# Top-k attention and a channel mixer on one core: all results turned back by the vector engine, match replacements written in place, one share of products moved in tail steps

## The chip, the cores and the metric

The kernel runs on one core of a Trainium2 chip. A core has a matrix engine (TensorE, here PE), a vector engine (VectorE, DVE), a scalar engine (ScalarE, ACT), a general engine (GpSimd, POOL), a queue that issues DMAs (SyncE, SP), and 16 DMA engines that all queues share. Each engine works through its own instructions in the order in which they were written; engines wait for one another by semaphores. The metric is the time of one execution on the device in microseconds (us). The kernel before takes 1773.88 us, the median of three runs (1771.52 to 1775.6).

## The reference

The inputs are q, k and v of 8 batches, 8 heads, 576 positions and 64 dimensions, and four weights U, V, w_ch1 and w_ch2, which arrive as float64. All the rest is float32.

```
scores = q @ k.T / 8                          # per batch and head, 576 x 576
kth    = the 32nd largest of each row
attn   = softmax over the entries >= kth      # the others count as 0
x      = attn @ v, heads side by side         # (8, 576, 512)
u      = x + (x.T @ U @ V).T                  # U: 576 x 32, V: 32 x 576
out    = u + relu(u @ w_ch1) @ w_ch2          # 512 -> 2048 -> 512
```

## The kernel before

**Steps.** Two heads of a batch form a group g, so there are 32 groups, four to a batch. The 576 rows of a group are cut into four tiles of 128 rows and a tail of 64 rows; the tails of the two heads share one tile. A step n is one tile t of one group: t = 0 to 3 are full steps with two chunks of 128 x 576 scores (one for each head), t = 4 is the tail step with one chunk. A batch is 20 steps, 16 full and 4 tail; in all there are 160.

**What a step does on DVE.** `front` finds the 32 largest of each row of each chunk. It takes the eight largest with `max` (line 385), and then three times overwrites those eight with a very negative number (`match_replace`, line 395) and takes the next eight (line 399). Each `match_replace` writes a new tile "rr" of which there are three buffers; a full step needs six. On the engine a replacement is two instructions, the load of the eight values and the replacement itself. In full steps from the 30th on, DVE also turns the second head's weights in blocks of 32 x 32 into a tile y (`blocks`, line 446). Four DMAs carry y to a scratch tile "away" in device memory (line 452) and one brings it back as part of the tile PT (line 456), so that it is fully transposed. The first head's weights are transposed on PE (line 474), whose results ACT copies into PT (lines 475 and 480).

**The other engines in a step.** ACT copies scores from PSUM to the tile Ssb and takes exponentials (line 351). POOL masks chunks (lines 402, 403 and 421). PE multiplies: scores (`scores`, lines 320 and 333, for the step that follows), weights with v (`values`, lines 498, 508 and 512; tile O), and four times a batch the mixing over positions (`mixed`, lines 533 to 566), which gives the tile uT.

**The channel products.** When a batch's four groups are mixed, `mlp(b)` is put in the list `fillers`. It is a generator that issues the matmuls of both channel products, one at a time (lines 581 and 600), and is advanced by `fill()`. Each call of `fill` adds a share to an account `due` and issues matmuls until the account is used up. The share is 1 in full steps and 0.65 in tail steps, and eight calls in each step use up one batch's products in 20 steps. So the products of batch b run among the attention steps of batch b + 1, and those of the last batch run alone at the end. The order of PE, ACT, DVE and POOL is the order of the calls in the main loop (from line 701 on): nothing is reordered there. The issues of SP are placed by the framework's scheduler.

**Where the results leave.** A batch's products are made for two spans of rows, of 320 and of 256, and for each span as four tiles "oT" of 128 channels. That makes eight tiles a batch, called tile 0 to tile 7 below. ACT copies a tile from PSUM (line 615) and POOL adds uT (line 616). Then `turned_back` transposes it, as rows of the output are positions and rows of oT are channels. It is put off in the list `late`: to the tenth matmul of the next tile, or to the fourth result of the next span, and for tile 7 to the moment at which the generator of that batch ends, with nothing put between. In the kernel before, batches 0 to 6 are turned on PE (line 648, two or three transposes a tile), ACT copies the result to "ob" (lines 650 and 652), and one or two DMAs write it (lines 654 and 659). Seven of the eight tiles of the last batch are turned by DVE instead, in blocks of 32 x 32 (line 630). There the DMAs put the blocks in place, 12 of them for a tile of 320 columns and 8 for one of 256 (lines 635 and 640), with pieces of 128 bytes in device memory.

**A main-loop step after the first batch** has this order (lines 775 to 807): four fills, with the PE transposes of the weights of an earlier step among them, `values(n - 2)`, `scores(n + 1)`, the first replacement round on DVE, a fill, the second round, the issue of y, two fills, the third round, and a last fill.

Of the kernel before, what the change touches and what calls it, by code (L numbers as in the profile page):

```python
# [8 lines left out]
F32 = mybir.dt.float32  # L9
# [17 lines left out]
def kernel(  # L27
# [29 lines left out]
    B, H, S, D = q.shape  # L57
    P = 128
# [3 lines left out]
    NF, NC = F // P, C // P  # L62
    NT, TAIL = 4, 64
# [19 lines left out]
    attn = ctx.enter_context(tc.tile_pool(name="attn", bufs=2))  # L83
# [11 lines left out]
    SPAN = ((0, 2 * P + TAIL), (2 * P + TAIL, S))  # L95
# [30 lines left out]
    def rows(t):  # L126
        return P if t < NT else TAIL
# [221 lines left out]
    def weigh(chunk, E, nmax, total=None):  # L349

        nc.scalar.activation(E, chunk, AF.Exp, bias=nmax, scale=SCALE, accum_out=total)  # L351

    def ways(g, t):

        if (g, t) == (NPAIR - 1, NT - 1):
            return (0,), (), (1,)
        if (g, t) == (NPAIR - 1, NT):
            return (0,), (), ()  # L360
        return (), (1,) if t < NT else (), (0,)
# [4 lines left out]
    def front(g, t):  # L366

        if t == 0:
            dens[g] = small.tile([P, 2 * NT + 1], F32, tag="den", name="den", bufs=3)
        chunks, den = S2s.pop((g, t)), dens[g]
        n = len(chunks)
        E2 = attn.tile([P, 2 * S], F32, tag="E", name="E", bufs=3)
        Es = [E2[:, c * S : (c + 1) * S] for c in range(n)]
        sums = [den[:, 2 * t + c : 2 * t + c + 1] for c in range(n)]
        probs[g, t] = E2
        curs, ms = list(chunks), [None] * n
        first = small.tile([P, 2, 8], F32, tag="first", name="first", bufs=3)  # L380
        nmax = small.tile([P, 2], F32, tag="nmax", name="nmax", bufs=4)
        order = (1, 0) if n == 2 else (0,)
        for c in order:
            ms[c] = first[:, c]
            nc.vector.max(ms[c], curs[c])  # L385
        yield
        early, pooled, gaps = ways(g, t)
        for i in range(1, TOPK // 8):
            if i == 1:
                nc.scalar.mul(nmax[:, 0:n], first[:, 0:n, 0], -SCALE)  # L390
                for c in early:
                    weigh(chunks[c], Es[c], nmax[:, c : c + 1])
            for c in order:
                nxt = attn.tile([P, S], F32, tag="rr", name="rr", bufs=3)
                nc.vector.match_replace(nxt, ms[c], curs[c], NEG)  # L395
                curs[c] = nxt
            for c in order:
                ms[c] = small.tile([P, 8], F32, tag="m8", name="m8", bufs=8)
                nc.vector.max(ms[c], curs[c])  # L399
            yield  # L400
        for c in pooled:
            nc.gpsimd.tensor_scalar(Es[c], chunks[c], ms[c][:, 7:8], NEG, ALU.is_lt, ALU.mult)  # L402
            nc.gpsimd.tensor_tensor(chunks[c], chunks[c], Es[c], ALU.add)  # L403
        for c in early:
            nc.vector.scalar_tensor_tensor(
                out=Es[c],
                in0=chunks[c],
                scalar=ms[c][:, 7:8],
                in1=Es[c],
                op0=ALU.is_ge,  # L410
                op1=ALU.mult,
                accum_out=sums[c],
            )
        if t == NT:
            del qkTs[g]
        yield
        for c in gaps:
            least = small.tile([P, 1], F32, tag="least", name="least", bufs=3)
            nc.scalar.mul(least, ms[c][:, 7:8], WIDEN)
            nc.scalar.activation(Es[c], chunks[c], AF.Relu, bias=least, scale=-WIDEN)  # L420
            nc.gpsimd.tensor_tensor(chunks[c], chunks[c], Es[c], ALU.subtract)  # L421
            yield
        ahead = pooled if shared(g, t) else ()
        for c in ahead:
            weigh(chunks[c], Es[c], nmax[:, c : c + 1], sums[c])
            yield
        for c in order:
            if c not in early and c not in ahead:
                weigh(chunks[c], Es[c], nmax[:, c : c + 1], sums[c])
        if t == NT and g != NPAIR - 1:  # L430
            nc.scalar.activation(den, den, AF.Identity, bias=eps)
        yield

    def shared(g, t):


        return t < NT and g * CH + t >= ROUNDED
# [183 lines left out]
    def turned_back(b, chunks, lo, c, oT):  # L621


        def run():
            cs = slice(c * P, (c + 1) * P)
            if b == B - 1 and (lo, c) != (SPAN[1][0], NC - 1):

                w = sum(rows(t) for t in chunks)
                ob = mlpp.tile([P, 3 * P], F32, tag="ob", name="ob", bufs=2)
                nc.vector.transpose(ob[:, 0:w], oT[:, 0:w])  # L630
                for a in range(4):
                    cs = slice(c * P + a * BLK, c * P + (a + 1) * BLK)
                    ba = ob[a * BLK : (a + 1) * BLK]
                    for t in chunks[0:2]:
                        nc.sync.dma_start(
                            out[b, 0:MAIN, cs].rearrange("(m i t) c -> t i m c", i=BLK, t=NT)[t],
                            ba[:, OFF[t] - lo : OFF[t] - lo + P].rearrange("i (m c) -> i m c", c=BLK),
                        )
                    if NT in chunks:
                        nc.sync.dma_start(  # L640
                            out[b, MAIN:S, cs].rearrange("(m i) c -> i m c", i=BLK),
                            ba[:, 2 * P : 2 * P + TAIL].rearrange("i (m c) -> i m c", c=BLK),
                        )
                return
            tp = ps_t.tile([P, 3, P], F32, tag="tp", name="tp")
            for i, t in enumerate(chunks):
                n = rows(t)
                nc.tensor.transpose(tp[0:n, i, :], oT[:, OFF[t] - lo : OFF[t] - lo + n], ident)  # L648
            ob = mlpp.tile([P, 3, P], F32, tag="ob", name="ob", bufs=2)
            nc.scalar.copy(ob[:, 0:2], tp[:, 0:2, :])  # L650
            if NT in chunks:
                nc.scalar.copy(ob[0:TAIL, 2], tp[0:TAIL, 2, :])
            t = chunks[0]
            nc.sync.dma_start(
                out[b, 0:MAIN, cs].rearrange("(p t) c -> p t c", t=NT)[:, t : t + 2, :],
                ob[:, 0:2],
            )
            if NT in chunks:
                nc.sync.dma_start(out[b, MAIN:S, cs], ob[0:TAIL, 2])

        return run
# [11 lines left out]
    def fill(k=1):  # L673


        nonlocal due
        for _ in range(k):
            if passes:
                passes.pop(0)()
            if mixing and next(mixing[0], True):  # L680
                mixing.pop(0)
            due += share * (SHORT if t == NT else 1) * (EARLY if n <= 2 * ALONE + 2 else 1)
            while due > 0:
                if not fillers:
                    due = 0.0
                    break
                done = next(fillers[0], None)
                if done is None:
                    fillers.pop(0)
                else:  # L690
                    due -= done
# [3 lines left out]
    t = 0  # L695
# [5 lines left out]
    for n in range(STEPS + 2):  # L701
        g, t = divmod(n, CH)
        if n < STEPS:
            if t == 0 and g + 1 < NP:
                load(g + 1)
            if t == 1 and g + 1 < NP:
                ready = prep(g + 1)
            fronts[n] = front(g, t)
            next(fronts[n])
# [70 lines left out]
            next(last)  # L780
        fill()
        next(turning, None)
        fill()
        if ease:
            next(last, None)
        if n - 2 >= ALONE:
# [17 lines left out]
        if t in (1, 3):  # L804
            next_params(1)
        next(here, None)
        fill()
    while mixing or fillers:
        fill()

# [30 lines left out]
```

## Time and profile before

| | before |
|---|---|
| time, median of three runs | 1773.88 us |
| span of the profiled execution | 1773.6 us |
| PE busy | 1669.3 us, 94% |
| DVE busy | 1560.3 us, 88% |
| ACT busy | 1029.4 us, 58% |
| POOL busy | 846.8 us, 48% |
| replacements on DVE (line 395) | 864, 742 ns each |
| transposes of results on PE (line 648) | 142, 25.3 us together |
| copies of them on ACT (lines 650, 652) | 85, 28.5 us together |
| transposes of results on DVE (line 630) | 7, 3.4 us together |

Shares of busy time mix stages, so they are read by stretches of the span. Until about 240 us the first batch's attention runs without channel products, with DVE busy 39.1 to 39.6 of each 40 us from 40 us on, and PE 19 to 36. From about 440 to 1632 us attention and channel products run together. From there to the end PE works alone on the last batch's products. A group of the profile is named by line, engine and operation, then the tile that is written and those that are read ("rr<-m,rr"); "mean ns" is the duration of one instruction. In the list of waits, "A <- B: 2.9, 4, 1.0" says that the instructions at A waited for B 2.9 us in all, in 4 waits, the longest 1.0.

### The profile page before, as it was taken

To read this page: it belongs to the slowest core of one execution; us is meant where nothing else is said; L and a number is where in the kernel's file an instruction comes from. 1 tells how busy PE (TensorE), PEld (TensorE's weight loads), DVE (VectorE), ACT (ScalarE), POOL (GpSimd) and SP (SyncE) were. 2 spreads that over 40 slices of the span, in tenths; PEclk is the share of its full clock that TensorE was granted. 3 is DMA by queue.
4 is the path that set the end of the run, shared out by engine and by line. 5 is a ranking of instruction groups with operands and counts; after the bars stand their busy time and mean duration, and the time that the engine had idled before them with its cause. 6 is when DMAs were issued, how large, how long until landed. Compare 5 with 4: busy or idle time off the path is not lost.

```text
span 1773.6 us, 28992 instructions
## 1 busy us (share of the span) xinstructions
PE 1669.3 (94%) x9851; PEld 1257.5 (71%) x9851; DVE 1560.3 (88%) x3106; ACT 1029.4 (58%) x2682; POOL 846.8 (48%) x591
## 2 busy tenths in 40 slices
PE   4666789999999999999999999999999999999999
PEld 2434556677777877788777877788777877788677
DVE  7999989899999999999999999999999999994000
ACT  4778777555656656565656656565656656564100
POOL 4777677535354554545445454444445444453000
PEclk7687799999999999999999999999999999999999
DMA  3222332222223332222233232232233232211010
GB/s 95 88 82 73 88 85 61 50 59 71 58 67 80 66 72 56 67 68 64 64 71 79 62 70 62 65 70 63 63 73 80 59 73 60 53 50 45 4 15 13
DMA packets 275829, 112.79 MB, mean 64 GB/s; under 512 B 173920, under 2 KB 260192, under 8 KB 275680
## 3 DMA queue, kind: packets, MB, share of 16 engines
q1 hardware_dynamic: 274624, 110.68, 26.4%
q8 instruction: 77, 1.26, 0.3%
q14 instruction: 72, 0.59, 0.1%
q10 hardware_dynamic: 1056, 0.26, 0.1%
HBM read 74.15 MB, written 36.70 MB: 63 GB/s over the span
## 4 chain that ended last, share of the span: by engine, by line
PE 75%; DVE 16%; POOL 4%; ACT 3%; issue 2%; DMA 1%; SPq 0%; POOLq 0%; DVEq 0%
PE mm L581 25%; PE mm L600 24%; DVE rr L395 7%; PE sc L333 6%; PE O L512 6%; DVE m L399 6%; PE tp L474 3%; DVE first L385 2%; PE sc L320 2%; PE O L498 2%; PE up L556 1%; PE O L508 1%; POOL E L402 1%; PE up L558 1%; PE tp L648 1%
## 5 line engine op out<-in xcount | busy, mean ns | idle before, releaser
L399 DVE MAX8 m<-rr 128x8 f32<-128x576 f32 x864 | 614.7, 748 | 5.5
L600 PE MATMUL mm<-hT,w 128*128 128x256 f32 (+1 forms) x2048 | 547.4, 410 | 0.0
L581 PE MATMUL mm<-uT,w 128*128 128x256 f32 (+1 forms) x2048 | 541.5, 410 | 0.9 <-ACT hT L593 0.9
L402 POOL TENSOR_SCALAR E<-Ssb,m 128x576 f32<-128x576 f32 x127 | 281.1, 2214 | 411.7 <-DVE m L399 409.1
L581 PEld LDWEIGHTS mm<-uT,w 128*128 128x128 f32 x2048 | 371.7, 190 | 115.1 <-issue 26.0
L600 PEld LDWEIGHTS mm<-hT,w 128*128 128x128 f32 x2048 | 368.3, 190 | 106.8 <-issue 22.5
L395 DVE MATCH_REPLACE8 rr<-m,rr 128x576 f32<-128x576 f32 x576 | 427.2, 742 | 0.0
L421 POOL TENSOR_TENSOR Ssb<-Ssb,E 128x576 f32<-128x576 f32 x159 | 225.4, 1418 | 122.3 <-ACT E L420 121.7
L351 ACT ACTIVATE E<-Ssb,nmax 128x576 f32<-128x576 f32 x288 | 223.3, 776 | 52.4 <-POOL Ssb L403 34.9
L593 ACT ACTIVATE hT<-mm 128x320 f32<-128x320 f32 (+1 forms) x256 | 105.1, 411 | 240.4 <-PE mm L581 240.1
L385 DVE MAX8 first<-Ssb 128x8 f32<-128x576 f32 x288 | 203.3, 742 | 31.4 <-ACT Ssb L346 31.4
L395 DVE MATCH_REPLACE8 rr<-first,Ssb 128x576 f32<-128x576 f32 x288 | 211.8, 742 | 0.0
L403 POOL TENSOR_TENSOR Ssb<-Ssb,E 128x576 f32<-128x576 f32 x127 | 179.3, 1412 | 10.6
L333 PE MATMUL sc<-qkT 64*128 64x288 f32 x1024 | 170.6, 454 | 6.7 <-ACT Ssb L344 5.8
L474 PE MATMUL tp<-ident,E 128*128 128x128 f32 x736 | 116.0, 283 | 37.1 <-ACT XT L521 14.6
L512 PE MATMUL O<-PT,va 128*64 128x128 f32 x2048 | 146.3, 284 | 1.9 <-DMA PT<-away 1.9
L474 PEld LDWEIGHTS tp<-ident,E 128*128 128x128 f32 x736 | 92.1, 145 | 68.7 <-ACT XT L521 16.6
L475 ACT COPY PT<-tp 128x512 f32<-128x512 f32 x184 | 106.6, 585 | 49.0 <-PE tp L474 46.4
L512 PEld LDWEIGHTS O<-PT,va 128*64 128x64 f32 x2048 | 113.7, 140 | 19.0 <-DMA PT<-away 2.9
L420 ACT ACTIVATE E<-Ssb,least 128x576 f32<-128x576 f32 x159 | 123.3, 776 | 5.2
L333 PEld LDWEIGHTS sc<-qkT 64*128 64x128 f32 x1024 | 93.3, 198 | 45.3 <-issue 14.3
L613 DVE TENSOR_TENSOR oT<-uT,mm 128x320 f32<-128x320 f32 (+1 forms) x8 | 3.6, 455 | 137.1 <-PE mm L600 137.1
(81 smaller groups left out, 1574.0 us busy)
## 6 DMA issues: line engine op xcount, KB each, us to landing
away<-y SPq DMA_DIRECT2D x416, 64.0 KB, 1.8
PT<-away SPq DMA_DIRECT2D x104, 256.0 KB, 2.8
raw<-in_moe_w_ch_dram SPq DMA_DIRECT2D x32, 512.0 KB, 3.8
va<-in_v_dram SPq DMA_DIRECT2D x64, 128.0 KB, 2.3
out_dram<-ob SPq DMA_DIRECT2D x57, 128.0 KB, 2.2
ld<-in_q_dram SPq DMA_DIRECT2D x108, 64.0 KB, 2.4
ld<-in_k_dram SPq DMA_DIRECT2D x108, 64.0 KB, 2.4
ld<-in_q_dram SPq DMA_DIRECT2D x108, 8.0 KB, 2.2
```

The source lines that it names most:

```text
L333: nc.tensor.matmul(sc[:, h, 0:HALF], lhsT=qkT[half(h), 0, cols(t)], rhs=qkT[half(h), 1, i * HALF : (i + 1) * HALF], start=True, stop=True,)
L351: nc.scalar.activation(E, chunk, AF.Exp, bias=nmax, scale=SCALE, accum_out=total)
L385: nc.vector.max(ms[c], curs[c])
L395: nc.vector.match_replace(nxt, ms[c], curs[c], NEG)
L399: nc.vector.max(ms[c], curs[c])
L402: nc.gpsimd.tensor_scalar(Es[c], chunks[c], ms[c][:, 7:8], NEG, ALU.is_lt, ALU.mult)
L403: nc.gpsimd.tensor_tensor(chunks[c], chunks[c], Es[c], ALU.add)
L421: nc.gpsimd.tensor_tensor(chunks[c], chunks[c], Es[c], ALU.subtract)
L474: nc.tensor.transpose(tp[:, j, :], E2[:, a : a + P], ident)
L512: nc.tensor.matmul(O[half(h)], lhsT=va[:, h, j, :], rhs=PB[:, j] if h and shared(g, t) else PT[:, NT * h + j], start=False, stop=(j == NT ...
L581: nc.tensor.matmul(ph[:, 0:w], lhsT=w1[:, cc, f * P : (f + 1) * P], rhs=uT[:, cc, lo:hi], start=(cc == 0), stop=(cc == NC - 1),)
L600: nc.tensor.matmul(po[:, 0:w], lhsT=w2[:, f, c * P : (c + 1) * P], rhs=hTs[f][:, 0:w], start=(f == 0), stop=(f == NF - 1),)
```

## The change

There are three edits.

1. `turned_back` takes the way over DVE for every tile of every batch, but for the last tile of the last batch. That is 56 tiles more on DVE, and as many fewer on PE and ACT.
2. In `front`, only the first replacement round of a step takes a new tile rr. Rounds two and three write into the tile that they read.
3. In the main loop after the first batch, a tail step leaves out the last of the four fills that stand ahead of `values` and `scores`, and makes two fills at its end where there was one.

```diff
             for c in order:
-                nxt = attn.tile([P, S], F32, tag="rr", name="rr", bufs=3)
+
+                nxt = attn.tile([P, S], F32, tag="rr", name="rr", bufs=3) if i == 1 else curs[c]
                 nc.vector.match_replace(nxt, ms[c], curs[c], NEG)
                 curs[c] = nxt
...
             cs = slice(c * P, (c + 1) * P)
-            if b == B - 1 and (lo, c) != (SPAN[1][0], NC - 1):
+            if (b, lo, c) != (B - 1, SPAN[1][0], NC - 1):
 
                 w = sum(rows(t) for t in chunks)
...
         fill()
         next(turning, None)
-        fill()
+        if t < NT:
+            fill()
         if ease:
             next(last, None)
         if n - 2 >= ALONE:
...
         next(here, None)
-        fill()
+        fill(1 if t < NT else 2)
     while mixing or fillers:
         fill()
```

## Prediction

> **What bounds the kernel now.** I read the page's busy times first, then stretches of 200 us, which are one batch each once the channel products run. The columns are the stretch, its length, then busy time and instructions of PE, PE's weight loads, DVE, ACT and POOL, then granted clock, DMA share, GB/s.
>
> ```profile
> 120.00:240.00 120.00, 86.21 (x519) 57.95 (x520) 118.17 (x242) 92.29 (x219) 88.38 (x62) 0.81 0.29 81
> 1000.00:1200.00 200.00, 199.88 (x1217) 152.58 (x1216) 193.94 (x385) 119.96 (x321) 95.96 (x64) 1.00 0.30 68
> 440.00:450.00 10.00, 8.08 (x48) 5.89 (x47) 9.93 (x22) 4.84 (x14) 4.05 (x4) 0.83 0.43 102
> ```
>
> In the first batch DVE is the bound. In the steady stretch PE is full (the list of waits has no wait of PE between 600 and 1600 us), yet DVE is only 6 us short of full. Its waits in the same stretch:
>
> ```profile
> DVE first L385 <- ACT Ssb L346: 2.9, 4, 1.0
> DVE y L446 <- ACT E L351: 0.7, 1, 0.7
> ```
>
> So of a period of 200.1 us (tile 7's copies on ACT start 200.1 apart), DVE alone needs 200.1 - 3.6 = 196.5. Two engines lie within 2%, and what links them decides. The timeline, cut to single instructions, shows the replacement rounds:
>
> ```profile
> 1002.52 0.74 DVE L395 MATCH_REPLACE8 rr<-first,Ssb 128x576 f32<-128x576 f32 x1
> 1003.24 0.74 DVE L395 MATCH_REPLACE8 rr<-first,Ssb 128x576 f32<-128x576 f32 x1
> 1005.29 0.74 DVE L395 MATCH_REPLACE8 rr<-m,rr 128x576 f32<-128x576 f32 x1
> 1006.14 0.74 DVE L395 MATCH_REPLACE8 rr<-m,rr 128x576 f32<-128x576 f32 x1
> ```
>
> In round one the two chunks' replacements start 0.72 us apart, in the later rounds 0.85. With three buffers the second chunk's new rr is the tile that the first chunk's replacement is still reading, so it waits for its end. Next, the end of a batch's products (tile 7), and the way of y to the matmul O that uses it:
>
> ```profile
> 1043.23 1.41 DVE L399 MAX8 m<-rr 128x8 f32<-128x576 f32 x2
> 1044.62 0.74 DVE L395 MATCH_REPLACE8 rr<-m,rr 128x576 f32<-128x576 f32 x1
> 1047.47 0.37 ACT L615 COPY oT<-mm 128x256 f32<-128x256 f32 x1 [0.49 <-PE mm L600]
> 1047.92 0.73 POOL L616 TENSOR_TENSOR oT<-oT,uT 128x256 f32<-128x256 f32 x1 [3.62 <-ACT oT L615]
> ...
> 1057.95 0.69 DVE L446 STREAM_TRANSPOSE y<-E 128x512 f32<-128x512 f32 x1
> 1058.67 2.75 SPq L452 DMA_DIRECT2D away<-y  x4
> 1062.95 0.34 SPq L456 DMA_DIRECT2D PT<-away  x1
> 1066.41 1.09 PE L512 MATMUL O<-PT,va 128*64 128x128 f32 x16
> ```
>
> PT lands 2.8 us after its issue (median), at 1065.75; its first reader, the second matmul pair of O, starts at 1066.5. The slack is 0.8 us, in a chain that starts on DVE. At the four other batch ends it is 0.2 to 1.9, with these 1.3 on average.
>
> **What the Trainium skill says.** "VectorE: DVE Perf Modes", section "Two Vector instructions with no wait between them": a held instruction starts only when the earlier ones have finished, one that is not held starts sooner; 0.85 against 0.72 us agrees. The same page, "The three transpose paths": VectorE transposes 32x32 blocks only, so the DMAs must place the blocks; the trace agrees (y, and ob's 8 or 12 DMAs). "TensorE: Matmul & The Clock Gate", "What's actually happening": a free-running window of 3413 ns watches PE, and an idle one halves the clock. The trace has it: after a wait of 1.9 us for tile 7 at 441.8 the clock is 0.83 over 10 us, which is 3.4 us at half. "DMA: Bandwidth & Descriptors", "Why small descriptors are slow (HBM only)": small pieces pay a fixed overhead each; with DMA share 0.30 no run here shows it to bind.
>
> **The change, part by part.** Prices of the results' way, from the answers on its tiles:
>
> ```profile
> L630 DVE STREAM_TRANSPOSE ob<-oT x7: 445/511/512, 1689.0 to 1762.9; 128x320 f32<-128x320 f32 x4, 128x256 f32<-128x256 f32 x3
> L635 SPq DMA_DIRECT2D out_dram<-ob x56: 315/430/436, 1689.5 to 1766.6; - x56
> 1020.31 0.36 PEld L648 LDWEIGHTS tp<-ident,oT 128*128 128x128 f32 x2
> 1020.64 0.30 PEld L600 LDWEIGHTS mm<-hT,w 128*128 128x128 f32 x2
> ```
>
> *PE.* A pair of result transposes takes PE 0.33 us (1020.31 to 1020.64), so 0.17 each. A batch has 20: 3.4 us. PE alone would need 196.7 a batch. ACT loses 85 copies less one (28 us); it is 60% busy, worth nothing by itself.
>
> *DVE, replacements in place.* With no shared buffer, I take round one's spacing for rounds two and three: 0.127 us a pair, 32 pairs a batch, 4.1 us. Bounds: nothing, if writing over the tile that is read costs as much, and 4.1. Tail steps have one chunk and gain nothing.
>
> *DVE, transposes.* Eight a batch, 4 x 0.51 + 4 x 0.45 = 3.8 us; y's transposes overlap their neighbours by 0.16 us, so at least 2.6. I take 3.2. DVE alone: 196.5 - 4.1 + 3.2 = 195.6.
>
> *SP.* A tile had one or two DMAs and has 12 or 8, of 0.43 us: 80 a batch, 34 us. SP has the room: it waits 97 us for y in 400 us. Where they go matters. They follow their DVE transpose, and y comes 5.6 us of DVE work or more after each of the first seven tiles, against 12 x 0.43 = 5.2; after tile 7 it comes 2.8 us later against 8 x 0.43 = 3.4, where PT has some 3 us of slack. Once, behind tile 1, y stands just ahead, and three DMAs fall between away and PT, where SP waits 1.3 us for away to land anyway. I take nothing in steady batches. In the first, one y follows tile 3 by 2.8 us with no slack at its PT (waits of 1.7 at O): up to 2 us.
>
> *DVE's new wait.* DVE takes tile 7's transpose between rounds one and two of a step. DVE is there at 1044.62 (the second pair of `max` of round one is done); POOL has the tile at 1048.65, as PE's last matmul ends at 1047.4. All of DVE stands behind it: two rounds, y, masks on POOL, exponentials on ACT. The other seven tiles are ready 2.8 us or more ahead of DVE. The y of the next step comes 4.0 + 0.4 (transpose) - 0.4 (three pairs) = 4.0 later. Its reader O stands in a tail step, which the third edit moves up by one fill. Alone, a batch's products take 124.2 us on PE (the last four pieces of the chain), and a tail fill is 0.65/(4 x 8 x 4.65) of it, 0.5 us. So O waits 4.0 + 0.5 - 1.3 = 3.2 us, against 3.1 saved by the 18 transposes from there to the next tile 7. The period comes to 200.1 + 3.2 - 3.1 = 200.2. That the waiting DVE later catches up does not help: PE has waited.
>
> *Third edit otherwise.* The same fills in a step; scores of tail steps 0.5 us sooner, so that DVE's 0.7 us waits there shrink. DVE isn't the bound, so nothing.
>
> **The sum**, against the profiled span of 1773.6 (the runs' median is 1773.9, so no correction). Until 238 us, DVE-bound: 34 pairs x 0.127 = -4.3. From there to the first tile 7 (443 us), where DVE, POOL and DMAs share the chain: PE saves 3, DVE 2, SP costs 2: 0 (-3 to +3). From the first tile 7 to the sixth: five periods, now 1005.2 (the first has the 1.9 us wait and the half clock), then 5 x 200.2 = 1001: -4.2. From the sixth to the end: O late by 2.3 (slack 1.9 there), the moved fill 0.5, transposes -3.4, and PE's wait of 1.3 at 1643 gone: -1.9. Sum -10.4: **1763 us**, 0.6% faster.
>
> **Rivals.**
> - *PE-bound throughout* (the chain behind tile 7 has more slack than I read). Five periods of 196.7 give -21.7, the start -7.4, the end -4.7: 1740, or up to 1750 with part of it. For: PE has no wait in 1000 us now. Against: slack of 0.2 to 1.9 us.
> - *The clock.* The 3.2 us of waiting fall on two O's some 9 us apart, about 1 and 2 us. If the second halves the clock for 3.4 us, PE loses 1.7 at each of six batch ends: 10 more, 1773. For: 1.9 us did it at 441.8. Against: 2.2 us at 262 did not.
> - *Slower: the result DMAs hold up y's.* The margin is 5.6 - 5.2 us; from 0.65 us per issue instead of 0.43, 12 take 7.8, and away and PT come over 2 us late, past the slack, at three y's a batch. At 3 us a batch for six batches beyond the forecast: 1781. For: SP's issues of four away DMAs take 2.75 us at times instead of 1.76. Against: DVE's saved time gives slack elsewhere.
> - *In place saves nothing*: 4.3 at the start and 0.4 a period lost, 1769.
>
> **How the numbers follow.** Forecast 0.46, PE-bound 0.18, clock 0.18, DMAs 0.13, in place 0.05. Under 0.2% (3.5 us) a measurement of this kernel can't tell from no change. Faster: 0.45 + 0.18 + 0.06 + 0.03 = 0.72; same 0.12; slower 0.16. The range leaves out half of PE-bound and most of the DMA case: 1744 to 1779. The forecast's own range is 1757 to 1768.
>
> **What would show it.** The later replacement pairs 0.72 us apart; line 648 with two instructions left; DVE waiting for POOL's line 616 about 4 us, once a batch; PE waiting at O (line 512) for PT once or twice a batch; periods of 200, not 197. It is wrong if PE shows no waits in the steady stretch, if clock drops stand behind each batch end, or if away's issue starts over 1 us after y ends.

## The result, and the profile after

The changed kernel takes 1781.53 us, the median of four runs (1781.14 to 1782.94), against 1773.36 for the kernel before (four runs, 1771.52 to 1775.6). The ratio is 1.0047 with a 95% interval of 1.003 to 1.0064: it is slower by half a per cent, where 1763 us were forecast. The profiled execution has a span of 1779.3 us, 5.7 more than before.

I take the same steps through the profile as before the change. Stretches of the span first (stretch, length, then busy time and instructions of PE, PE's weight loads, DVE, ACT, POOL, then granted clock, DMA share, GB/s):

```profile
1000.00:1200.00 200.00, 197.38 (x1187) 148.96 (x1186) 192.12 (x390) 116.07 (x307) 95.96 (x64) 1.00 0.31 67
446.00:456.00 10.00, 7.17 (x31) 4.69 (x29) 10.00 (x22) 2.40 (x7) 3.57 (x2) 1.00 0.36 77
456.00:466.00 10.00, 9.73 (x47) 6.16 (x47) 9.83 (x21) 5.66 (x14) 4.75 (x4) 0.83 0.36 78
```

PE was full in the steady stretch (199.88 of 200) and now is not: it lost 2.5 us, and it executes 30 instructions fewer in the same time. So PE did get less work, and yet the batch became longer. The lower two rows are the end of the first batch's products: a hole in PE, and behind it the clock at half for about 3.4 us. The kernel before had such a hole and such a drop too, some 10 us earlier.

The list of waits of the steady stretch, 1000 to 1200 us (total, times, longest), begins for PE, which had no wait here before, with

```profile
PE O L513 <- DMA PT<-away: 2.4, 2, 2.1
```

and for DVE with a line that is new as well:

```profile
DVE ob L631 <- POOL oT L617: 3.2, 1, 3.2
```

It is one wait at tile 7, once a batch; the two kinds of wait that DVE had before follow with 2.2 and 1.2 us. The timeline shows how it gets from there to PE:

```profile
1046.30 1.41 DVE L400 MAX8 m<-rr 128x8 f32<-128x576 f32 x2
...
1050.13 0.73 POOL L617 TENSOR_TENSOR oT<-oT,uT 128x256 f32<-128x256 f32 x1 [3.25 <-ACT oT L616]
1050.89 0.45 DVE L631 STREAM_TRANSPOSE ob<-oT 128x256 f32<-128x256 f32 x1 [3.19 <-POOL oT L617]
1051.37 4.93 SPq L636 DMA_DIRECT2D out_dram<-ob  x8
...
1054.01 0.69 DVE L447 STREAM_TRANSPOSE y<-E 128x512 f32<-128x512 f32 x1
1056.40 1.82 SPq L453 DMA_DIRECT2D away<-y  x4
1059.75 0.34 SPq L457 DMA_DIRECT2D PT<-away  x1
1062.49 1.09 PE L513 MATMUL O<-PT,va 128*64 128x128 f32 x14 [2.11 <-DMA PT<-away]
```

DVE ends the first round of a step at 1047.7 and stands until POOL has added uT at 1050.86. Then it transposes the tile, and y follows later than it would have. SP has eight result DMAs in front of y's four, so away starts 1.70 us after y's end (1054.70). PT comes late, and PE waits 2.11 us at O. This is the longest of these waits. At the four other batch ends between 600 and 1500 us DVE stands as long (3.2 us each), and PE's longest wait behind it is 0.8 to 1.7 us.

The replacements did what was forecast. The timeline of DVE, a later round of a full step:

```profile
1000.39 0.74 DVE L396 MATCH_REPLACE8 rr<-m,rr 128x576 f32<-128x576 f32 x1
1001.12 0.74 DVE L396 MATCH_REPLACE8 rr<-m,rr 128x576 f32<-128x576 f32 x1
```

The pair starts 0.73 us apart, as a first round's does, where it stood 0.85 apart before. The duration of one (0.74) is the same, so the gain shows only in the starts.

Where the 5.7 us of the span come from is read from tile 7, whose copy on ACT marks the end of each batch's products:

| | before | after | forecast change | change |
|---|---|---|---|---|
| first matmul of the products | 217.0 | 212.4 | -4.3 | -4.6 |
| first tile 7 | 442.5 | 442.3 | -4.3 | -0.2 |
| first period | 204.28 | 204.18 | -4.1 | -0.1 |
| next four periods | 800.97 | 806.95 | -0.2 | +6.0 |
| from the sixth tile 7 to the end | | | -1.9 | 0 |
| span | 1773.6 | 1779.3 | -10.4 | +5.7 |

The first row is a part of the second, and the last one the sum of the other four, up to rounding.

The forecast is missed by 4.1 us in the first batch, 4.0 in the first period, 6.2 in the four steady ones and 1.9 at the end.

### The profile page after: what moved, and what is told of

It is laid out like the page before. It is cut to its first block, busy times and chain, and to the rows that moved or that the text cites. A ratio compares the mean times of both kernels' runs of the same rounds, so it can differ in the third digit from the quotient of the medians.

```text
span 1779.3 us, 29149 instructions
## 1 busy us (share of the span) xinstructions
PE 1661.9 (93%) x9711; PEld 1243.6 (70%) x9711; DVE 1560.6 (88%) x3162; ACT 1004.5 (56%) x2598; POOL 846.7 (48%) x591
## 4 chain that ended last, share of the span: by engine, by line
PE 71%; DVE 16%; POOL 4%; ACT 3%; DMA 3%; SPq 2%; issue 1%; DVEq 0%; POOLq 0%
PE mm L582 24%; PE mm L601 24%; DVE rr L396 7%; PE sc L333 6%; DVE m L400 6%; PE O L513 5%; PE tp L475 3%; DVE first L385 2%; PE O L499 2%; PE sc L320 1%; DMA PT<-away 1%; PE up L557 1%; PE O L509 1%; POOL E L403 1%; PE up L559 1%
## 5 line engine op out<-in xcount | busy, mean ns | idle before, releaser
L513 PE MATMUL O<-PT,va 128*64 128x128 f32 x2048 | 151.1, 284 | 14.4 <-DMA PT<-away 14.4
```

The source lines that it names most:

```text
L513: nc.tensor.matmul(O[half(h)], lhsT=va[:, h, j, :], rhs=PB[:, j] if h and shared(g, t) else PT[:, NT * h + j], start=False, stop=(j == NT ...
```

## Experiments

All times are medians of device time; the ratio is to the kernel before, run on the same chip. "Period" is the time from one tile 7 to the next, from the profiled execution, the first one apart, and then the mean of the next four.

| kernel | us | ratio, interval | first tile 7 | periods |
|---|---|---|---|---|
| after | 1781.53 | 1.0047 [1.003, 1.0064] | 442.3 | 204.18; 201.74 |
| tile 7 on PE | 1765.69 | 0.9947 [0.9935, 0.996] | 442.0 | 201.00; 199.12 |
| tile 7 put off | 1765.35 | 0.9945 [0.9933, 0.9958] | 442.3 | 201.59; 198.91 |
| tile 7 without DMAs | 1782.95 | 1.0042 [1.0028, 1.0056] | 442.2 | 204.31; 202.27 |
| in place alone | 1765.82 | 0.9949 [0.9937, 0.9962] | 436.6 | 202.38; 200.12 |
| results on DVE alone | 1798.97 | 1.0134 [1.012, 1.0147] | 448.1 | 207.05; 203.95 |
| third edit alone | 1778.37 | 1.0014 [1.0008, 1.0021] | 442.5 | 204.15; 200.66 |
| after without third edit | 1780.7 | 1.0032 [1.0023, 1.0041] | 442.0 | 204.81; 201.48 |
| put off, no third edit | 1761.13 | 0.9918 [0.9905, 0.9932] | 442.1 | 200.70; 198.74 |
| put off, no result DMAs | 1756.27 | 0.9894 [0.9879, 0.991] | 436.6 | 200.92; 198.49 |
| put off, first batch on PE | 1757.37 | 0.9899 [0.9885, 0.9912] | 435.3 | 201.57; 198.81 |
| put off, DMAs on ACT's queue | 1895.76 | 1.068 [1.0666, 1.0695] | 453.7 | 222.45; 219.13 |

### Is it DVE's wait at tile 7, or the eight DMAs behind it?

Tile 7 of every batch back on PE:

```diff
-            if (b, lo, c) != (B - 1, SPAN[1][0], NC - 1):
+            if (lo, c) != (SPAN[1][0], NC - 1):
```

> The changed kernel, but tile 7 of every batch is turned on PE as before (the other seven stay on DVE). Theory (DVE's stand before tile 7, and tile 7's eight DMAs ahead of away, cost PE 2.9 us at O once a batch): both are gone, PE saves its 18 transposes a batch at 0.11 us each, periods of about 198.1 us between tiles 7 instead of 201.6, and about 1760 us in all. Rival (the 48 other transposes on DVE and the DMAs in small pieces are what costs): periods stay above 200.5, time 1775 to 1781.

Tile 7 stays on DVE, but is put off to the fourth result of the next batch's products, as the fourth tile of the first span already is; the list `late` is now one for all batches:

```diff
-        late = []
...
-        late.pop()()
+        if b == B - 1:
+            late.pop()()
...
-    fillers, mixing, due = [], [], 0.0
+    fillers, mixing, due, late = [], [], 0.0, []
```

> The changed kernel, but tile 7 of batches 0 to 6 is turned on DVE at the fourth result of the next batch's products, as the fourth tile of the first span is, and not at once. Theory (it is the wait for a tile that is not ready that costs, not the transpose): no wait of DVE for POOL, periods of about 197.9 us, 1759 us in all. Rival (all 56 transposes and their DMAs cost, wherever they stand): periods of 200.5 or more, 1775 to 1781.

DVE waits and transposes as in the changed kernel, but no DMA follows for tile 7 of batches 0 to 6:

```diff
+                if b < B - 1 and (lo, c) == (SPAN[1][0], NC - 1):
+                    return
```

> The changed kernel without the eight DMAs of tile 7 in batches 0 to 6 (that part of the output isn't written); DVE's transpose and its wait stay. Theory A (the DMAs ahead of away are what makes PT late behind tile 7): no wait at the first O behind it, and at the tail step's O a wait of 2.4 us or less; periods of 198.5 to 200.5, time 1763 to 1775. Theory B (DVE's wait alone is enough): periods of 201 to 201.6, time 1778 to 1781.

The first two gain 1.0% on the changed kernel (0.9947 and 0.9945 against 1.0047); the third gains nothing that shows (1.0042, with an interval that overlaps). Both came out some 6 us above what was expected, with periods of 199 and not 198, and the third just above its theory B. Both ways to take DVE's wait off nearly clear PE's list of waits: from 480 to 1440 us, with four batch ends, it has 1.0 us with tile 7 on PE and 0.5 us with tile 7 put off, against 7.9 in the changed kernel (6.4 for PT at O and 1.5 for ACT's copies).

Where the loss lies is seen when the matmuls of PE are laid side by side, one by one. From 2 to 30 us behind each of the first six tiles 7 the changed kernel falls 2.3 to 3.1 us behind the one with tile 7 put off, 16.5 us together. Their spans differ by 17.1.

Without the eight DMAs the chain runs as follows (timeline):

```profile
1054.73 0.69 DVE L447 STREAM_TRANSPOSE y<-E 128x512 f32<-128x512 f32 x1
1055.45 1.77 SPq L453 DMA_DIRECT2D away<-y  x4
...
1061.51 1.09 PE L513 MATMUL O<-PT,va 128*64 128x128 f32 x14 [0.43 <-DMA PT<-away]
...
1070.47 0.49 PE L509 MATMUL O<-PT,vd 128*128 128x128 f32 x2 [0.62 <-ACT PT L481]
1071.62 1.09 PE L513 MATMUL O<-PT,va 128*64 128x128 f32 x14 [0.29 <-DMA PT<-away]
```

Away now starts at once when y ends, and the first O waits 0.43 us instead of 2.11. But the next O waits too, on both of its inputs, and the period is no shorter. DVE had lost 3.19 us here too, and PE pays for it either at one O or at two. So away's late issue, which the prediction had named as a sign that it is wrong, is there in the changed kernel and costs nothing of its own that shows in the time. Put off, the tile costs DVE no wait. Had I read only the changed kernel's timeline, the eight DMAs would have looked like the cause.

### Each edit alone

Only the second edit, rounds two and three in place:

```diff
-                nxt = attn.tile([P, S], F32, tag="rr", name="rr", bufs=3)
+                nxt = attn.tile([P, S], F32, tag="rr", name="rr", bufs=3) if i == 1 else curs[c]
```

> The kernel before with the replacements in place alone. Later pairs start 0.73 us apart instead of 0.85. In the first batch DVE is the bound, so 4.3 us should be saved by 235 us; afterwards PE is the bound and nothing more is saved: 1769 us. Rival (the first saving is lost again before PE becomes the bound, as in the changed kernel, where PE was 4.7 us ahead at 235 us and 1.8 behind at 474): 1772 to 1774.

Only the first edit, all results on DVE:

```diff
-            if b == B - 1 and (lo, c) != (SPAN[1][0], NC - 1):
+            if (b, lo, c) != (B - 1, SPAN[1][0], NC - 1):
```

> The kernel before with the first edit alone (DVE turns the results, no replacement in place, no share moved). Theory: the wait behind tile 7 costs about 3 us a batch as in the changed kernel and nothing is saved at the start; later replacement pairs stay 0.85 us apart, so DVE needs 196.5 + 3.2 = 199.7 us a batch by itself and gives PE no slack elsewhere either: periods of 201.5 to 203, time 1784 to 1792. Rival (the third edit is what makes O too early): periods of about 200, time 1775 to 1780.

Only the third edit:

```diff
-        fill()
+        if t < NT:
+            fill()
...
-        fill()
+        fill(1 if t < NT else 2)
```

> The kernel before with the third edit alone. DVE's waits in tail steps (2.9 us in 200) shrink, and O of the tail steps comes 0.5 us sooner. PE is the bound, so the period stays at 200.1 and the time within 2 us of before, if PT has 0.5 us of slack at every tail step; it has between 0 and 2, so up to 0.5 us lost at a third of the 28 tail steps: 1773 to 1778. Rival (it does what it says, and scores sooner save time): 1768 or less.

And the changed kernel with the third edit undone:

```diff
-        if t < NT:
-            fill()
+        fill()
...
-        fill(1 if t < NT else 2)
+        fill()
```

> The changed kernel without the third edit: tile 7 is still turned at once on DVE. By e6_shift_only the third edit costs 0.5 us a batch, and by e7 against e2 4.2 us in all; by the sum behind tile 7 it takes 0.5 us of PT's slack. Expected: periods of 201.1 and 1777 to 1779. Rival (the third edit pays where DVE is late, since scores come sooner): 1783 or more.

*In place* is worth 9 us alone, twice the 4.3 us that were expected, and neither of the two expectations had it. In the profiles all of it falls before the third tile 7: the first comes 5.9 us sooner, the first period is 1.9 shorter and the second 0.5. The wait behind the first tile 7 is 1.4 us there and not 1.9, and no half clock follows it. After that all periods are 200.12, as before, since PE is the bound there.

*Results on DVE alone* costs 1.3%, more than all three edits together and more than the 1784 to 1792 us that were expected. Without the replacements' gain DVE has no room left, and PE waits for what DVE makes. The list of PE's waits from 480 to 1640 us begins with

```profile
PE O L512 <- DMA PT<-away: 13.6, 13, 2.6
```

So the second edit is what pays for the first.

*The third edit alone* costs 0.54 us in every steady period. Its time lies just above the range expected. The list of waits of PE's weight loads from 600 to 1600 us has a line that the kernel before does not have:

```profile
PEld O L508 <- ACT PT L480: 6.4, 20, 0.3
```

Twenty waits of 0.3 us are one for each tail step of five batches. The timeline of one of them:

```profile
1066.07 0.30 PEld L508 LDWEIGHTS O<-PT,vd 128*128 128x128 f32 x2 [0.32 <-ACT PT L480]
```

O's first weight load needs ACT's copy of the transpose just ahead of it. In the kernel before, the share of products that the edit leaves out stands between the two (timeline of before, four weight loads of line 581):

```profile
1064.91 0.84 PEld L581 LDWEIGHTS mm<-uT,w 128*128 128x128 f32 x4
1065.22 0.27 ACT L480 COPY PT<-tp 128x128 f32<-128x128 f32 x1
1065.83 0.46 PEld L508 LDWEIGHTS O<-PT,vd 128*128 128x128 f32 x2
```

The move put the share where nothing waits, and took it from where it covered a copy. Laid side by side with the kernel before, PE of the kernel with the third edit alone falls back 0.07 to 0.19 us at each tail step of a period and nowhere else, 0.54 together. The rest of the 0.3 us that a weight load waits does not show in the matmuls. The cost is not the same in every version. Undoing the edit in the changed kernel gives 0.15% (1.0032 against 1.0047, with intervals that overlap, so this is not clear of noise) and 0.26 us a period on average, where that kernel's periods range from 200.5 to 203.2; its 1780.7 us lie between the range expected and the rival's. With tile 7 put off it gives 0.27% (0.9918 against 0.9945), but only 0.17 us a period. Only where the edit stands alone is its place shown.

### What do the result DMAs cost, and how fast can it be?

Tile 7 put off and the third edit undone:

> The kernel of e2_late7 without the third edit. There PE saves 2.0 us a period by fewer transposes and loses 1.0 of it, most of it (0.5 to 0.9) at the O of the tail step behind tile 2. Theory A (the third edit takes 0.5 us of PT's slack there): periods of 198.2 to 198.6, time 1760 to 1763. Theory B (the DMAs of tile 2 hold back away there): periods of 199 as in e2_late7, 1764 to 1767.

Tile 7 put off, and the DMAs of all results of batches 0 to 6 left out:

```diff
+                if b < B - 1:
+                    return
```

> The kernel of e2_late7 with the result DMAs of batches 0 to 6 left out (that part of the output isn't written). It shows what all of them cost together, in the first batch (where in e2_late7 four of them stand between away and PT at 408 us, O then waits 2.4 us and the clock drops) and later. Theory B: tile 7 of the first batch is reached at about 437 us instead of 442, periods of 198.0, time 1753 to 1757. Theory A: periods of 199 stay, and only the start is better: 1759 to 1762.

Tile 7 put off, third edit undone, and the first batch's results on PE:

```diff
-            if (b, lo, c) != (B - 1, SPAN[1][0], NC - 1):
+            if b > 0 and (b, lo, c) != (B - 1, SPAN[1][0], NC - 1):
```

> The kernel of e7_late7_no_shift, but the first batch's results are turned on PE. Theory (in the first batch the result DMAs on SP stand ahead of away or PT where PT has no slack, and from the second batch on they do not): tile 7 of the first batch is reached at about 437 us instead of 442, periods of 198.6 after it, time 1755 to 1758. Rival (the loss at the start isn't from there): 1760 to 1763.

Tile 7 put off, third edit undone, and the result DMAs issued from ACT's queue instead of SP's:

```diff
-                        nc.sync.dma_start(
+                        nc.scalar.dma_start(
```

> The kernel of e7_late7_no_shift with the results' DMAs issued from ACT's queue and not from SP's. Theory (SP's order is what costs): SP is free, the first batch ends at 437 us; but ACT has 34 us a batch of issues more and waits for each DVE transpose in its own order. If ACT's issues cost it little: 1754 to 1758. If ACT's queue holds up the exponentials and copies behind it: PE waits for ACT, 1770 or more.

With tile 7 put off and no third edit the time, 1761.13 us, fits theory A, but the period of 198.74 lies in the range of neither theory. Of the other three, the first two came out in the range of their theories, and ACT's queue far on the slow side.

Leaving the result DMAs out gains 9 us (0.9894 against 0.9945). Of these, 5.7 lie before the first tile 7 (436.6 against 442.3) and 0.4 in each steady period. So the DMAs cost little in steady batches and much in the first. With the first batch on PE the first tile 7 comes 6.7 us sooner, though ACT has its copies again. Laid side by side with the kernel without result DMAs, PE in the one that has them falls back mainly at two places of the first batch: 3.0 us between 355 and 364, and 2.6 between 406 and 412. The timeline of the changed kernel at the first:

```profile
354.46 1.83 SPq L453 DMA_DIRECT2D away<-y  x4
...
360.39 1.97 PE L513 MATMUL O<-PT,va 128*64 128x128 f32 x14 [2.89 <-DMA PT<-away]
```

This is the place that the prediction had named. Here y is ready at 352.16, but the twelve DMAs of tile 3 stand in SP's order ahead of away, and away starts 2.3 us late. O waits 2.89 us, against 0.74 without result DMAs, and the clock is at half for 6.8 us and not 3.4. The second place:

```profile
404.40 3.00 SPq L453 DMA_DIRECT2D away<-y  x4
...
408.16 1.75 SPq L636 DMA_DIRECT2D out_dram<-ob  x4
410.14 0.34 SPq L457 DMA_DIRECT2D PT<-away  x1
...
412.70 1.97 PE L513 MATMUL O<-PT,va 128*64 128x128 f32 x14 [2.78 <-DMA PT<-away]
```

Four result DMAs stand in SP's order between away and PT. Their tile is transposed only at 408.14, and SP takes them until 409.91 with PT behind them. PT could not have gone at once, as it needs away, whose DMAs land 1.8 us (median) after their issue; from the end of away's issues (407.40) that is about 409.2, an estimate. Away's own issues take 3.00 us here where four take 1.77 at other times, but that is not the result DMAs' doing: without them they take 2.64 at this place. There O waits 1.38 us instead of 2.78, and the clock stays full, where it halves at 412 in the changed kernel.

ACT's queue makes it 6.8% slower, for a plain reason. The Trainium skill's "DMA: Bandwidth & Descriptors", section "Issuing engines are not separate DMA queues", says that issuing from a second engine saves only issue time on the sequencer. Here the sequencer is one with copies to do. A tile's 12 issues hold ACT for 5.8 us (1007.41 to 1013.21). Issuing does not count as busy, so ACT's list of waits, over the whole span, has

```profile
ACT PT L476 <- DMA out_dram<-ob: 91.8, 18, 6.7
```

PE in turn waits 61 us for ACT from 480 to 1440 us, and not once for the DMA of PT.

The version with the first batch on PE is the fastest that keeps all results: 1757.37 us (1756.96 to 1757.77), 1.0% faster than before and, by the ratios, 1.5% faster than the changed kernel.

## Why the prediction was wrong, step by step

From the ratios, in units of the kernel before (1775 us), the time of the changed kernel is put together thus: in place -9.1 (0.9949); the way over DVE with tile 7 put off -5.5 (0.9949 to 0.9918); tile 7 at its place in the change +20.2 (0.9918 to 1.0032); the third edit +2.7 (1.0032 to 1.0047). The sum is +8.3. Each ratio is known to about 2 us, and the shares of the last two depend on their order: with the third edit taken first they are +4.8 and +18.1.

- **Replacements in place: right.** Forecast -4.3 us until the products begin, measured -4.6, and 0.73 us between starts as in round one. A single profile is good to a microsecond or two here: the ten versions with the rounds in place reach that point at 212.0 to 214.7 us, the three without at 216.4 to 217.0, which is 3.6 apart on average.
- **DVE's wait at tile 7: right in kind and size.** Forecast a wait of 4.0 and 3.2 us lost on PE; DVE's wait was 3.19, and PE, compared instruction by instruction with before, fell 2.9 us further behind between 1049 and 1058 (2.2 to 5.1). Behind this tile 7 it fell almost wholly on one O and not on two, because of the DMAs.
- **A transpose of results on PE at 0.17 us: wrong, it is 0.11.** This is the first term of the sum to fail. I took 0.33 us for a pair from the starts of weight loads on both sides of it, and that interval holds the time of the next load as well. Compare a stretch with the transposes and one without, from the first weight load of a group of 14 to the first load behind it. Before (timeline of the weight loads), with three of them:

```profile
936.88 1.38 PEld L600 LDWEIGHTS mm<-hT,w 128*128 128x128 f32 x6
938.34 0.49 PEld L648 LDWEIGHTS tp<-ident,oT 128*128 128x128 f32 x3
938.83 1.92 PEld L600 LDWEIGHTS mm<-hT,w 128*128 128x128 f32 x8
940.82 0.63 PEld L474 LDWEIGHTS tp<-ident,E 128*128 128x128 f32 x4
```

And after, with none:

```profile
940.37 3.53 PEld L601 LDWEIGHTS mm<-hT,w 128*128 128x128 f32 x14
943.98 0.63 PEld L475 LDWEIGHTS tp<-ident,E 128*128 128x128 f32 x4
```

  That is 3.94 us against 3.61: 0.33 for three. The pair that the prediction read as 0.33 us adds 0.22, when PE's matmuls before and with tile 7 put off are laid side by side. The 18 transposes that were to pay for the wait save 2.0 us and not 3.1, and the 20 of a batch 2.2 and not 3.4. The kernel without result DMAs agrees: 200.12 - 2.2 + 0.54 for the third edit is 198.46, and its periods are 198.49. The version with tile 7 put off and no third edit should have 197.9 and has 198.74; PE loses 0.1 to 0.4 us there at several O's. The Trainium skill's "TensorE: Matmul & The Clock Gate", "Part 4: PE-mode transpose", has about 275 ns for one of bf16 in a kernel's context. These fp32 ones agree as to their duration (273 ns, median of line 648), but what one adds to a full stream of products is 0.11 us.
- **The third edit "otherwise nothing": wrong, 0.54 us a period where it stands alone.** I asked what gets sooner and whom it helps, and not what the share had stood in front of. With both terms the steady period comes to 200.1 + 2.9 - 2.0 + 0.5 = 201.5; measured 201.74.
- **SP, nothing in steady batches: nearly right** (0.4 us a period). **Up to 2 us in the first batch: wrong.** The result DMAs cost 5.7 there. The stretch up to the first tile 7, forecast at 0, gave back 4.4 of the 4.6 us gained. The one y that follows a tile closely cost 3.0 (with tile 7 put off), the time at half clock included. The second place, with result DMAs between away and PT, was not in the sum; it cost 2.6.
- **The first period: wrong.** I let the wait and half clock behind the first tile 7 go and set a steady period. They went at tile 7 itself, and came back in the next 15 us as a wait of 2.6 us at O with a half clock behind it. In all changed versions the first period is 1.9 to 3.5 us longer than those that follow (4.0 before the change), those without DVE's wait included. With tile 7 put off PE still waits 1.2 to 1.9 us there, at the O's behind tile 7; what the rest is stays open.
- **The end: wrong by 1.9.** It had the same transposes at 0.17 us (3.4 for 2.2), and PE fell 3.0 us back behind the sixth tile 7 where the sum had 2.3. (That 2.3 does not follow from the delay of 4.0 and the slack of 1.9, which give 2.1.)
- **The rivals.** PE-bound throughout is out for the changed kernel: PE has waits in the steady stretch. The clock is out in the steady batches of this profile: waits of up to 2.1 us leave it at 1.00 from 480 to 1640 us. It is not out altogether: in the changed kernel without the third edit, a wait of 1.75 us at 659 halves it once. In place saving nothing is out. The slower case named 1781 us, and the time fell there, but its mechanism, result DMAs that push y's past their slack at three y's a batch, does not: leaving all of them out gains 0.4 us a period and not 3. Its number was right by luck, through other terms.

The error was one of balance: the forecast set a loss of 3.2 us against a gain of 3.1, both from single readings, and put nothing on the two being a third apart. The range of 1744 to 1779 ended 2.5 us short.

## What to carry to other kernels

When an engine takes over work whose input comes from the engine that is the bound, look for the one instance that is not ready when its turn comes: here seven tiles of eight cost little in steady batches, and the eighth cost 1.1% until it was put off. What an instruction costs in a full stream is read from two stretches, one with it and one without, not from the starts around it. Before moving filler work, ask what wait it covers where it stands. Where two profiles run the same instructions in the same order, laying them side by side shows at which place the time is lost.

## What the runs showed of the hardware that I had not expected

- A transpose of 128 x 128 fp32 on PE between products adds 0.11 us at six of a batch's eight tiles, although its weight load alone shows as 0.16 (0.49 for three).
- Issues of DMAs on SP with the same shape take very different times: the median is 0.43 us, the longest 1.7, and eight in a row took 4.93 us behind tile 7 where eight medians are 3.4. The result DMAs are not what makes away's issues slow: four of them take over 2.5 us 12 times of 104 with tile 7 put off, and 14 times with the result DMAs left out as well.
- How long PE waits does not decide alone whether the clock halves. Waits of 2.53 and 2.56 us did not do it (at 237 us, with tile 7 on PE and with the rounds in place alone), while 1.75 us did (at 659 us, changed kernel without the third edit) and so did 1.9 before the change. The last two are shorter than the window of 3413 ns that the prediction quotes. Each stretch at half between 240 us and the end of the products lasts 3.4 us or two or three times that.
